# Two loads move behind two transposes, and 14 short idle products become 6 long ones

## The chip, the cores and the metric

The kernel runs on one core of a Trainium2 chip. The metric is the device time of one execution in microseconds. All times below are microseconds unless ns is written. The core has TensorE (PE, with its weight loads as PEld), VectorE (DVE), ScalarE (ACT), GpSimd (POOL) and SyncE (SP), each with an instruction stream of its own that it takes in order, and 16 DMA engines. A DMA is issued from one of the streams; here nearly all come from SyncE's.

## What is computed

Eight batches of retention (attention with a decaying causal mask, no softmax) with 8 heads, 576 positions and 64 values a head, and behind it a two-layer network over the 4608 tokens, in which the activation is a "snake":

```python
scores = scale * np.matmul(q, k.transpose(0, 1, 3, 2))
Dmat = np.where(rel >= 0, gamma[:, None, None] ** rel[None, :, :], 0.0)
attn = np.matmul(scores * Dmat, v)                 # (8, 8, 576, 64)
x = attn.transpose(0, 2, 1, 3).reshape(4608, 512)
h = x @ w_in                                       # (4608, 2048)
s = np.sin(alpha * h)
out = (h + s * s / (alpha + 1e-09)) @ w_out        # (4608, 512)
```

Inputs and output are float32; the kernel computes in float16 with float32 sums.

## The kernel before

**Tiles.** The first 512 positions of each batch form one block of 512 tokens; the last 64 positions of all batches form a ninth block. A batch's q, k and v come in two parts of 256 positions (`p` = 0, 1), each a float32 tile "raw" of 128 x 1024, in 512 KB. `load(b, nm, p)` issues one such load from SyncE (L148). `cast(b, nm, p, eng)` multiplies it by the decay factors into a float16 tile, on VectorE or GpSimd (L194; v is only copied, L121 or L119).

**Retention of a batch.** `crossed(b, p, nms)` issues a DMA transpose of the cast k or q from SyncE (L217), which gives the tiles kT and qT. `scores` multiplies kT and qT on TensorE (L372, 16 narrow products a call), and `masked` applies the decay mask on VectorE (L384). `outer` makes the sums of k times v for the four chunks of 128 positions (L308, narrow products), `evict` copies them to the tile kvs on ScalarE (L119), `more(c)` adds up the state from chunk to chunk on GpSimd (two instructions, L353 and L354), and `to_state(c)` writes the float16 state: on GpSimd (L346; for chunk 3 into the tile sS, which the ninth block uses) or on ScalarE (L344). There is one buffer kvs for all batches. `values` (L414) and `add_states` (L436) make the output of the batch, and `keep` copies it to xT.

**The network.** `project(n, fc, tag)` multiplies xT of block n with 128 columns of w_in in four wide products (L549) into the PSUM bank that the tag names. `sine` (L557, ScalarE), `square` (L568 on VectorE or GpSimd, L566 on ScalarE: the sine's output times itself) and `product` (L573, VectorE) make the activation gT; the product is the last reader of the bank, so the next project with the same tag waits for it. `gemm2` multiplies gT with w_out, four wide products a call (L592), and `finish(n, c, eng)` copies 128 tokens of output to osb (L119 or L121) and stores them in two DMAs from SyncE (L585).

**Order.** Up to the end of block 2's projections the order is written out by hand, call by call, in the program's text (L653 to L1131); after that a loop places the work of the later batches between the 16 units of each block (L1135 on). Each engine, and SyncE with its DMAs, works through its own instructions in the order of the text. Two places matter here.

At the start, `keep_busy(n, tag, m)` gives TensorE n products of m columns of zeros (L605), whose result nobody reads. One such call stands between the cast of the first q and its transposes on TensorE (`turn`, L227), which write to the same bank "h2".

In the middle (L994 to L1044), batch 3's retention starts while block 1's output and block 2's projections are under way. SyncE's stream there holds, in this order: the transposes of batch 3's second half, the loads of batch 4's k (second half) and q (first half), the transposes of batch 3's first half, the stores of block 1's output parts 1 and 0, and the loads of batch 4's k (first half), q (second half) and v. GpSimd's stream holds: the casts of batch 3's k (first half, in two parts), `more(3)` of batch 2, the casts of the two loads named, `to_state(3)` of batch 2, then `more(1)` to `more(3)` of batch 3 with their states. VectorE's holds: the two masks of batch 3's second half, the copy for `finish(1, 1)`, square and product of (2, 3) and of (2, 1), the mask of part (0, 1), square and product of (2, 7), the products of (2, 2) and (2, 11), and the cast of batch 4's q (second half). ScalarE's holds: the sines of (2, 3) and (2, 1), `evict` of batch 3 into kvs, the copy for `finish(1, 0)`, and the next sines.

Of the kernel before, what the change touches and what calls it, by code (L numbers as in the profile page):

```python
# [35 lines left out]
def kernel(  # L36
# [68 lines left out]
    V, A_, G_ = nc.vector, nc.scalar, nc.gpsimd  # L105
# [8 lines left out]
    def halves(n):  # L114
        return slice(64 * n, 64 * n + 64)
# [10 lines left out]
    def place(tag, shape, dtype):  # L126

        name = tag + next(slot_of[tag])
        if name not in places:
            places[name] = work.tile(shape, dtype, tag=name, bufs=1, name=name)  # L130
        return places[name]
# [5 lines left out]
    def load(b, nm, p):  # L137
        if p < 2 and b >= HALVED and nm != "q":
            t_ = place("raw", [P, H, 2 * D], F32)
            for g in range(2):  # L140
                for r in range(2):
                    s0 = 256 * p + 128 * g + 64 * r
                    nc.sync.dma_start(
                        t_[halves(g), :, r * D : r * D + D], src[nm][b, :, s0 : s0 + 64, :].rearrange("h i d -> i h d")
                    )
        elif p < 2:
            t_ = place("raw", [P, H, 2 * D], F32)
            nc.sync.dma_start(  # L148
                t_, src[nm][b, :, 256 * p : 256 * p + 256, :].rearrange("h (i r) d -> i h (r d)", r=2)
            )  # L150
        else:
            if b % 2 == 0:
                raw[b, nm, 2] = work.tile([P, H, D], F32, tag="raws", bufs=3, name=nm + "s32")
            t_ = raw[b - b % 2, nm, 2]
            nc.sync.dma_start(t_[halves(b % 2)], src[nm][b, :, 512:576, :].rearrange("h i d -> i h d"))
        raw[b, nm, p] = t_
# [47 lines left out]
    def new_T(b, nm, p):  # L204
        if (b, nm, p) not in T:
            T[b, nm, p] = (
                place(nm + "T", [P, 8, P], F16)
                if p < 2
                else work.tile([P, 4, P], F16, tag=nm + "Ts", bufs=B // 2, name=nm + "Ts")
            )  # L210
        return T[b, nm, p]

    def crossed(b, p, nms="kq"):
        for nm in nms:
            x = half[b, nm, p]
            x = x.rearrange("p a r t d -> p (a r t d)") if p < 2 else x.rearrange("p a t d -> p (a t d)")
            nc.sync.dma_start_transpose(new_T(b, nm, p), x)  # L217
# [363 lines left out]
    def finish(n, c, eng=None, cols=slice(0, 512), issue=(nc.sync, nc.sync)):  # L581
        osb = work.tile([P, 512], F32, tag="osb", bufs=4, name="osb")
        copy(eng or nc.scalar, osb[:, cols], ops[n, c, cols.start][:, cols])
        for r in range(2):
            issue[r].dma_start(rows_of(n, c)[r, :, cols], osb[halves(r), cols])  # L585

    def gemm2(n, u, tag, cols=slice(0, 512)):
        c, part = divmod(u, 4)
        if (n, c, cols.start) not in ops:
            ops[n, c, cols.start] = psum.tile([P, 512], F32, tag=tag, bufs=1, name="ops")  # L590
        for fk in range(4 * part, 4 * part + 4):
            matmul(  # L592
                ops[n, c, cols.start][:, cols], gT[n][:, fk, c * P : (c + 1) * P], w_out16[:, fk, cols],
                start=(fk == 0), stop=(fk == FC - 1), skip_group_check=True,
            )
# [6 lines left out]
    def keep_busy(n, tag, m=512):  # L602
        idle = psum.tile([P, 512], F32, tag=tag, bufs=1, name="idle")
        for _ in range(n):
            matmul(idle[:, 0:m], zero[:, 0:P], zero[:, 0:m], start=True, stop=True)  # L605
# [46 lines left out]
    with tc.manual_schedule():  # L652
# [20 lines left out]
        at[0].take_sum(0, A_)  # L673
        at[0].to_state(0, A_)
        cast(0, "q", 0, V)
        keep_busy(14, "h2", 200)
        at[0].next_sum(1)
        at[0].to_state(1, A_)
        load(0, "k", 1)
# [314 lines left out]
        at[2].more(3)  # L994
        crossed(3, 1, "k")
        crossed(3, 1, "q")
        load(4, "k", 1)
        cast(4, "k", 1, G_)
        load(4, "q", 0)
        cast(4, "q", 0, G_)  # L1000
        at[3].scores(1, 1, "m1")
        at[3].masked(1, 1)
        at[3].scores(1, 0, "m0")
# [3 lines left out]
        at[3].masked(1, 0)  # L1007
        crossed(3, 0, "k")
        crossed(3, 0, "q")
        gemm2(1, 7, "h1")  # L1010
        finish(1, 1, V)
        project(2, 1, "h0")
# [243 lines left out]
```

## Time and profile before

| | us |
|---|---|
| median of 3 runs | 306.36 |
| lowest, highest | 305.94, 307.76 |
| the profiled execution, its own time | 307.47 |
| its span, first to last instruction | 305.8 |
| TensorE busy in the span | 291.5 |
| VectorE, ScalarE, GpSimd busy | 199.9, 193.2, 128.7 |

The mean granted clock of TensorE is 0.998. In the lines of the trace, a row of a timeline gives the start, the time it took, the engine, the line of the kernel, the operation, the tiles written and read, the shape and the count of instructions merged; in brackets stand the idle time of the engine before it and what ended that. "SPq" is SyncE's stream, whose rows are DMA issues: their time is that of issuing, not of the transfer. "issue" means a wait without a cause in the profile. The end of a product in a row is modelled and includes its way through the array, so a next product can start before it.

### The profile page before, as it was taken

Reading aid. Unit: us, or ns where it says so; the run is one execution under the profiler, and the core shown is the slowest. Engines: PE = TensorE matmul, PEld = TensorE weight load, DVE = VectorE, ACT = ScalarE, POOL = GpSimd, SP = SyncE. Lnnn points to the kernel's source line nnn. Section 1 sums busy time; section 2 is a strip of 40 time slices with the busy share of each in tenths; the row PEclk is TensorE's granted clock in tenths of the full one; section 3 lists DMA queues with packets and bytes.
Section 4 is the critical chain, followed back from the end, with each engine's and each line's share of the span. In section 5 each row is a group of like instructions: output and inputs, shape, how many; then the busy total and the mean of one; then the engine's idle time right before and its main releaser. Section 6 shows DMA issues by size and latency. Waiting matters only on the chain.

```text
span 305.8 us, 7881 instructions
## 1 busy us (share of the span) xinstructions
PE 291.5 (95%) x3217; PEld 155.8 (51%) x3217; DVE 199.9 (65%) x281; ACT 193.2 (63%) x323; POOL 128.7 (42%) x149
## 2 busy tenths in 40 slices
PE   3879999999899999999999999999999999999995
PEld 1658555545444644554456444545455454444443
DVE  2877786978776876767667766566656746555600
ACT  3749886995378668664776577746774556555411
POOL 2767672468574555786159626743030000000000
PEclk9999999999999999999999999999999999999999
DMA  8999999998957379989799969966351121111232
GB/s 220 347 226 213 261 270 304 292 272 166 221 150 212 82 168 193 255 182 145 170 259 161 204 147 274 172 138 156 87 121 39 39 45 35 36 34 34 48 88 73
DMA packets 115620, 49.98 MB, mean 163 GB/s; under 512 B 71424, under 2 KB 110592, under 8 KB 115584
## 3 DMA queue, kind: packets, MB, share of 16 engines
q1 hardware_dynamic: 112064, 45.10, 62.5%
q0 software_dynamic: 2688, 4.19, 7.6%
q8 instruction: 25, 0.41, 0.6%
q10 hardware_dynamic: 832, 0.18, 0.4%
q14 instruction: 11, 0.09, 0.1%
HBM read 36.75 MB, written 9.44 MB: 151 GB/s over the span
## 4 chain that ended last, share of the span: by engine, by line
PE 83%; DMA 9%; DVE 3%; issue 2%; SPq 1%; ACT 1%; POOL 1%; DVEq 0%; POOLq 0%; ACTq 0%
PE ops L592 38%; PE hps L549 37%; DMA w_in<-in_moe_w_in_dram 3%; PE o L414 2%; PE sc L372 2%; DMA raw<-in_k_dram 2%; DMA raw<-in_q_dram 2%; DMA raw<-in_v_dram 2%; PE kv L308 1%; SPq L148 1%; PE o L436 1%; DVE ss L568 1%; DVE gT L573 1%; POOL k L194 1%; DVE ret L384 0%
## 5 line engine op out<-in xcount | busy, mean ns | idle before, releaser
L592 PE MATMUL ops<-w_out,gT 128*128 128x512 f16 (+2 forms) x592 | 142.8, 374 | 0.9 <-issue 0.7
L557 ACT ACTIVATE s<-hps,alpha_t 128x512 f16<-128x512 f32 x144 | 97.6, 684 | 67.3 <-PE hps L549 66.2
L573 DVE SCALAR_TENSOR_TENSOR gT<-ss,inva,hps 128x512 f16<-128x512 f16 x144 | 105.5, 745 | 52.5 <-ACT ss L566 48.1
L549 PE MATMUL hps<-xT,w_in 128*128 128x512 f16 (+1 forms) x544 | 126.8, 367 | 0.3 <-DMA w_in<-in_moe_w_in_dram 0.2
L549 PEld LDWEIGHTS <-w_in 128*128 128x128 f16 x608 | 67.9, 114 | 56.7 <-issue 1.0
L592 PEld LDWEIGHTS <-gT 128*128 128x128 f16 x592 | 56.3, 98 | 63.9 <-issue 1.7
L568 DVE TENSOR_TENSOR ss<-s 128x512 f16<-128x512 f16 x62 | 37.1, 598 | 18.0 <-ACT s L557 17.4
L566 ACT ACTIVATE ss<-s 128x512 f16<-128x512 f16 x73 | 46.0, 631 | 1.4
L194 POOL TENSOR_TENSOR k<-raw,cn 128x1024 f16<-128x1024 f32 (+1 forms) x17 | 26.6, 1574 | 38.0 <-DMA raw<-in_k_dram 30.5
L119 ACT COPY osb<-ops 128x512 f32<-128x512 f32 (+1 forms) x33 | 19.2, 580 | 15.3 <-PE ops L592 14.0
L384 DVE TENSOR_TENSOR ret<-sc,mask 128x1024 f16<-128x1024 f32 x20 | 23.8, 1218 | 4.2 <-PE sc L372 4.1
L194 POOL TENSOR_TENSOR q<-raw,cn 128x1024 f16<-128x1024 f32 (+1 forms) x10 | 18.2, 1837 | 3.4 <-DMA raw<-in_q_dram 3.4
L354 POOL TENSOR_TENSOR kvs<-s,kvs 128x256 f32<-128x256 f32 x21 | 16.6, 790 | 3.6 <-ACT kvs L119 2.3
L353 POOL TENSOR_TENSOR s<-kvs,cn 128x256 f32<-128x256 f32 x21 | 12.8, 612 | 8.6 <-ACT kvs L119 8.4
L121 POOL CAST v<-raw 128x1024 f16<-128x1024 f32 (+1 forms) x11 | 11.0, 997 | 13.0 <-DMA raw<-in_v_dram 13.0
L549 PE MATMUL hps<-xS,w_in 128*128 128x512 f16 x64 | 16.4, 379 | 0.0
L119 ACT CAST xT<-o 128x1024 f16<-128x1024 f32 (+1 forms) x13 | 12.7, 986 | 5.4 <-PE o L436 5.3
L568 POOL TENSOR_TENSOR ss<-s 128x512 f16<-128x512 f16 x9 | 9.3, 1037 | 8.6 <-ACT s L557 8.6
L119 ACT COPY kvs<-kv 128x512 f32<-128x512 f32 (+2 forms) x14 | 8.0, 573 | 7.4 <-PE kv L308 5.1
L178 POOL TENSOR_TENSOR ks<-ks,cn 128x512 f16<-128x512 f32 x4 | 4.2, 1042 | 19.8 <-DMA vs<-in_v_dram 12.3
L372 PE MATMUL sc<-qT,kT 64*64 64x128 f16 (+1 forms) x512 | 10.6, 215 | 1.8 <-DVE ret L384 1.0
L414 PE MATMUL o<-ret,v 64*64 64x128 f16 (+1 forms) x512 | 11.4, 215 | 0.8 <-issue 0.3
(57 smaller groups left out, 153.2 us busy)
## 6 DMA issues: line engine op xcount, KB each, us to landing
out_dram<-osb SPq DMA_DIRECT2D x70, 128.0 KB, 2.5
raw<-in_q_dram SPq DMA_DIRECT2D x16, 512.0 KB, 5.9
raw<-in_k_dram SPq DMA_DIRECT2D x10, 512.0 KB, 6.1
raw<-in_v_dram SPq DMA_DIRECT2D x10, 512.0 KB, 5.9
raw<-in_v_dram SPq DMA_DIRECT2D x24, 128.0 KB, 3.4
raw<-in_k_dram SPq DMA_DIRECT2D x24, 128.0 KB, 3.3
w_in<-in_moe_w_in_dram POOLq DMA_DIRECT2D x4, 512.0 KB, 11.5
w_out<-in_moe_w_out_dram POOLq DMA_DIRECT2D x4, 512.0 KB, 11.7
```

Of the source, the lines that this page charges most:

```text
L119: eng.copy(d_, s_)
L194: eng.tensor_tensor(dst[:, a0:a1].rearrange("p a r t d -> p t (a r) d"), t_.rearrange("p (t a) x -> p t a x", t=2)[:, :, a0:a1].rearrange( ...
L354: nc.gpsimd.tensor_tensor(self.kvs[:, c], s32, self.kvs[:, c], ADD)
L372: matmul(sc[halves(g), t, c : c + n], kT[halves(t), 2 * a + r, halves(g)], qT[halves(t), 2 * a : 2 * a + 2, 64 * g + i0 : 64 * g + 64], st ...
L384: nc.vector.tensor_tensor(ret.rearrange("p t (z x) -> p (t z) x", z=2)[:, :, 0:n], sc.rearrange("p t (z x) -> p (t z) x", z=2)[:, :, 0:n], ...
L414: made.append(matmul(o[t][halves(e), c : c + 128].rearrange("p (r i) -> p r i", r=2)[:, :, i0:64], v16[halves(g), 4 * t + 2 * x + e, r, :] ...
L549: matmul(hps_of[n, fc][0][:, cols], w_in16[fc // 4][:, a, fc % 4 :: 4], xs[n][:, a, cols], start=(a == 0 and part != 1), stop=(a == KT - 1 ...
L557: nc.scalar.activation(s_t, hps, mybir.ActivationFunctionType.Sin, bias=0.0, scale=alpha_t[:, fc : fc + 1],)
L566: nc.scalar.activation(ss_t, s_t, mybir.ActivationFunctionType.Square)
L568: eng.tensor_tensor(ss_t, s_t, s_t, MULT)
L573: nc.vector.scalar_tensor_tensor(gT[n][:, fc, :], ss_t, inva[:, fc : fc + 1], hps, MULT, ADD)
L592: matmul(ops[n, c, cols.start][:, cols], gT[n][:, fk, c * P : (c + 1) * P], w_out16[:, fk, cols], start=(fk == 0), stop=(fk == FC - 1), sk ...
```

## The change

Two edits. The first swaps, in the text of the order, two loads of batch 4 with their casts on GpSimd against what stood between them and `gemm2(1, 7)`: they now come behind the two DMA transposes of batch 3's first half, and on GpSimd behind `to_state(3)` of batch 2. The buffers that they use stay the same. The second replaces 14 idle products of 200 columns by 6 of 467.

```diff
         at[0].to_state(0, A_)
         cast(0, "q", 0, V)
-        keep_busy(14, "h2", 200)
+        keep_busy(6, "h2", 467)
         at[0].next_sum(1)
...
         at[2].more(3)
         crossed(3, 1, "k")
         crossed(3, 1, "q")
-        load(4, "k", 1)
-        cast(4, "k", 1, G_)
-        load(4, "q", 0)
-        cast(4, "q", 0, G_)
         at[3].scores(1, 1, "m1")
         at[3].masked(1, 1)
         at[3].scores(1, 0, "m0")
         at[2].to_state(3, G_)
         project(2, 3, "op")
         sine(2, 3)
         at[3].masked(1, 0)
         crossed(3, 0, "k")
         crossed(3, 0, "q")
+        load(4, "k", 1)
+        cast(4, "k", 1, G_)
+        load(4, "q", 0)
+        cast(4, "q", 0, G_)
         gemm2(1, 7, "h1")
         finish(1, 1, V)
         project(2, 1, "h0")
```

## The prediction

> **What bounds the kernel now.** I read the page first: the engines' shares and the DMA queues.
>
> ```profile
> span 305.8 us, 7881 instructions
> ...
> PE 291.5 (95%) x3217; PEld 155.8 (51%) x3217; DVE 199.9 (65%) x281; ACT 193.2 (63%) x323; POOL 128.7 (42%) x149
> ...
> q8 instruction: 25, 0.41, 0.6%
> ```
>
> TensorE is busy for 95% of the span. So an edit pays only if it removes a place where TensorE stands still, or makes one. The moved loads lie between 72 and 97 us, so next I read the chain of work that ended last for that stretch, and then each engine's timeline in it.
>
> ```profile
> 82.22 1.79 DVE ss L568
> ...
> 88.04 5.56 DMA raw<-in_q_dram
> ...
> 93.79 1.22 DVE q L194
> ...
> 101.03 0.54 PE kv L308 x64
> ```
>
> The chain leaves TensorE here. It runs through a VectorE square that took 1.79 us and, later, through the load of batch 4's q (second half), which VectorE must cast before it can make its next product. What TensorE lost by it is seen in its own timeline.
>
> ```profile
> 82.09 0.71 PE L308 MATMUL kv<-v,k 64*64 64x64 f16 x64
> 83.65 0.42 PE L372 MATMUL sc<-qT,kT 64*64 64x128 f16 x16 [0.85 <-DMA qT<-q]
> 84.00 2.98 PE L549 MATMUL hps<-xT,w_in 128*128 128x512 f16 x12
> 86.81 3.62 PE L592 MATMUL ops<-w_out,gT 128*128 128x512 f16 x16
> 90.27 3.62 PE L549 MATMUL hps<-xT,w_in 128*128 128x512 f16 x16
> 93.72 1.89 PE L592 MATMUL ops<-w_out,gT 128*128 128x512 f16 x8
> 95.72 1.02 PE L549 MATMUL hps<-xT,w_in 128*128 128x512 f16 x4
> 96.68 0.42 PE L414 MATMUL o<-ret,v 64*64 64x128 f16 x16
> ```
>
> Sixteen wide products go from 90.27 to the next start at 93.72: 0.216 each, with nothing lost. With that step the standstills are: 83.65 - (82.09 + 0.54 for 64 narrow products, the chain's row of 101.03) = 1.02; 86.81 - (84.00 + 12 x 0.216) = 0.22; 95.72 - (93.72 + 8 x 0.216) = 0.27; 96.68 - (95.72 + 4 x 0.216) = 0.10. Their sum, 1.6 us, is the most that moving the loads can give here.
>
> **The change, part one: two loads move behind two transposes.** First SyncE's queue, which the four transfers share.
>
> ```profile
> 68.52 1.25 SPq L217 DMA_TRANSPOSE qT<-q  x1
> ...
> 74.82 0.58 SPq L148 DMA_DIRECT2D raw<-in_k_dram  x1
> ...
> 76.12 2.93 SPq L217 DMA_TRANSPOSE kT<-k  x1
> 79.14 2.39 SPq L217 DMA_TRANSPOSE qT<-q  x1
> ```
>
> Then GpSimd, whose stream also holds the two casts that move.
>
> ```profile
> 72.34 2.04 POOL L194 TENSOR_TENSOR k<-raw,cn 128x512 f16<-128x512 f32 x2
> ...
> 75.03 0.72 POOL L354 TENSOR_TENSOR kvs<-s,kvs 128x256 f32<-128x256 f32 x1
> 79.27 1.90 POOL L194 TENSOR_TENSOR k<-raw,cn 128x1024 f16<-128x1024 f32 x1 [3.51 <-PE sc L372]
> 81.82 1.90 POOL L194 TENSOR_TENSOR q<-raw,cn 128x1024 f16<-128x1024 f32 x1 [0.65 <-DMA raw<-in_q_dram]
> 83.68 0.80 POOL L346 TENSOR_TENSOR sS<-kvs,cn 128x256 f16<-128x256 f32 x1
> 85.60 0.61 POOL L353 TENSOR_TENSOR s<-kvs,cn 128x256 f32<-128x256 f32 x1 [1.13 <-ACT kvs L119]
> ```
>
> *Transposes.* Their source, batch 3's first half of k, is cast by 74.38 (72.34 + 2.04), so the first can issue at 74.82, where the load now does. A transpose right behind another took 1.25 (68.52) to 2.39 (79.14) of the queue. Two of them are issued by 77.3 to 79.6, instead of 81.53 (79.14 + 2.39). TensorE could use them at 82.63. The old issue, done at 81.53, let the scores start at 83.65, 2.1 later; with the upper row this is 81.7. So the wait of 1.02 goes with either.
>
> *Loads.* They issue from 77.3 to 79.6 on, instead of 74.82. The k load reached its cast 4.45 after its issue (74.82 to 79.27), the q load 2.55 behind it (81.82). So k comes at 81.8 to 84.1 and q at 84.3 to 86.6. I take 82.3 and 84.9: nearer the lower end, since 68.52 is a transpose with no load ahead of it, as these will be, but not at it, since a longer issue is as common.
>
> *GpSimd's order.* The state of batch 2 (sS) now comes ahead of the casts and runs at 75.8 (75.03 + 0.72) instead of 83.68. ScalarE waited for it:
>
> ```profile
> 84.51 1.02 ACT L119 COPY kvs<-kv 128x1024 f32<-128x1024 f32 x1 [1.63 <-POOL sS L346]
> 85.42 0.59 ACT L119 COPY osb<-ops 128x512 f32<-128x512 f32 x1
> ...
> 88.98 1.05 ACT L344 ACTIVATE s<-kvs,cn 128x64 f16<-128x64 f32 x4
> 91.33 0.69 ACT L557 ACTIVATE s<-hps,alpha_t 128x512 f16<-128x512 f32 x1 [1.30 <-PE hps L549]
> ```
>
> That copy of kvs can now start at about 82.9, when the 64 products are done. What follows in ScalarE's order comes 1.6 earlier: the copy of the output block (85.42 to 83.8), SyncE's stores of it, and behind these the load of 88.04, now at 86.4. VectorE's cast of that q moves from 93.79 to 92.2, and the standstills of 0.27 and 0.10 are covered. What is late next: the state sums, queued on GpSimd behind the two casts, start at 84.9 + 1.9 = 86.8 instead of 85.60, at the upper end at 88.5. A sum is two instructions (0.61, and 0.72 as at 75.03), done by 89.9 at the latest. ScalarE needs it for the work of 88.98, which would shift by 0.9, and 1.30 of idle time follow: no cost.
>
> *VectorE.* Here lies the price.
>
> ```profile
> 82.14 1.86 DVE L568 TENSOR_TENSOR ss<-s 128x512 f16<-128x512 f16 x1
> 84.04 0.75 DVE L573 SCALAR_TENSOR_TENSOR gT<-ss,inva,hps 128x512 f16<-128x512 f16 x1
> 84.70 0.42 DVE L568 TENSOR_TENSOR ss<-s 128x512 f16<-128x512 f16 x1
> 85.16 0.75 DVE L573 SCALAR_TENSOR_TENSOR gT<-ss,inva,hps 128x512 f16<-128x512 f16 x1
> ```
>
> The same square takes 0.42 at 84.70 and 1.86 at 82.14. The long one lies under GpSimd's cast of 81.82 to 83.72 and ends 0.28 after it: it waited for the cast. The product behind it, done at 84.79, frees the bank for the 5th of the wide products of 84.00, and the next one, done at 85.91, that for the 9th. So with the DMA wait gone TensorE still meets these two. The Trainium skill ("SBUF — State Buffer", section "Who interferes with whom") has this as a rule: a VectorE instruction with two SBUF inputs and a GpSimd instruction that reads SBUF exclude each other for the whole instruction, and the first to start wins. The trace agrees at 82.14.
>
> So the sum turns on who starts first. With k's cast at 82.3 the square passes ahead of it (82.14 to 82.56) and its product ends at 83.4. The second square meets that cast (82.3 to 84.2), ends at 84.5, and its product at 85.2. TensorE makes the scores at 82.63, four products from 83.0 and four from 83.87, is ready for the 9th at 84.73 and waits 0.5 until 85.25. Of 1.6 remain 0.5: gain **1.1**. Bounds: 1.6 gained, if k lands after 83.4 and both squares pass first; 1.2 lost, as the first rival works out.
>
> **Part two: 14 idle products of 200 columns become 6 of 467.**
>
> ```profile
> 8.27 2.52 PE L605 MATMUL idle<-zero 128*128 128x200 f16 x14
> 10.84 0.61 PE L227 MATMUL tr<-ident,q 128*128 128x128 f16 x8
> ```
>
> 2800 columns become 2802; at 2.52 us for 2800 the six take the same time, and the transposes behind them still start at 10.84. These eight take 0.61 together, the clock is up by then, and with the same busy time ahead it should be so again. Cost 0. What remains is that TensorE's stream has 8 products and 8 weight loads fewer, and the trace shows where this may count.
>
> ```profile
> 19.27:196.09 176.82, 174.17 (x2168) 94.55 (x2168) 130.96 (x175) 127.19 (x214) 105.95 (x114) 1.00 0.91 208
> ```
>
> ```profile
> 19.28 0.36 PE L414 MATMUL o<-ret,v 64*64 64x128 f16 x11 [0.30 <-issue]
> ```
>
> ```profile
> 194.13 1.24 PE L592 MATMUL ops<-w_out,gT 128*128 128x512 f16 x5
> 196.10 0.81 PE L592 MATMUL ops<-w_out,gT 128*128 128x512 f16 x3 [0.72 <-issue]
> ```
>
> Two waits of TensorE have no releaser ("issue"). The one at 196.10 costs 196.10 - (194.13 + 5 x 0.216) = 0.89. The instruction queue moved 25 packets, 0.41 MB / 25 = 16.4 KB each, and 6434 products and loads / 25 make 257 to a packet. Between the two waits lie 2 x 2168 = 4336 of them: 17 packets of 255. So both waits stand at a seam between two blocks of instructions. With 16 instructions fewer ahead, the second seam falls 16 later in the code, behind 8 more wide products: it is reached at 195.21 + 8 x 0.216 = 196.94. The block was there at 196.10 and is asked for a few tenths later at most, so the wait goes: gain **0.89**. Bounds: 0, if the block comes later too, and a loss of the same 0.89, if another seam lands badly. The seam of 19.28 moves by 8 short products, a tenth or two: 0.
>
> **Sum.** 1.1 + 0.89 = 2.0 off the profiled execution's 307.47 (span 305.8 and 1.7 around it) gives 305.5. That execution is 1.1 above the median of 306.36, so against the median: **304.4**.
>
> **Rivals.**
> *The cast comes first, twice.* If k lands by 82.0, its cast takes 82.0 to 83.9 and holds the first square until 84.2; that product ends at 84.95. If q then lands by 84.6, its cast (to 86.5) holds the second square until 86.8 and the product until 87.5. TensorE, ready at 83.87, waits 1.1, then, ready at 85.85, 1.7: 2.8 against 1.6, a loss of 1.2. With the seam's gain: 306.36 + 1.2 - 0.89 = 306.7, slower than before. It decides where k lands: before or after 82.14, and my 82.3 is barely past it. For it: the lower row gives 81.8. Against: 2.39 is seen for a transpose behind another too (79.14).
> *The seam stays.* The wait at 196.10 has another cause, or turns up elsewhere: 306.36 - 1.1 = 305.3. The Trainium skill ("Runtime: NRT & Kernel Launch", section "Instruction fetch mechanics") has blocks of 256 instructions and calls the cost of crossing from one to the next mostly hidden. By that rule the shorter stream is worth nothing; the 0.89 speaks against it.
> *The loads come late.* With 2.93 (76.12) for each transpose, q lands near 87.7, the sums end past 91, and ScalarE's next sine starts 0.8 late: taken as the whole gain of part one, 305.5.
>
> **How the numbers follow.** Likeliest (square first, seam gone) 0.45: 304.4, own range 303.8 to 304.9. Cast first 0.22: 306.7. Seam stays 0.11: 305.3. Loads late 0.07: 305.5. Beyond these, waits that I did not see, 0.15. The range 303.5 to 307.1 holds the likeliest, the two milder rivals and nearly all of the first: 8 in 10. Over 1% (about what a measurement of this kernel can tell from no change) is below 303.3 or above 309.4. The four priced cases stay inside that, and even their upper bounds together (1.6 + 0.89 = 2.5) do. So the tails are the 0.15 and a little of the cases' own: 0.12 faster, 0.07 slower, 0.81 within.
>
> **What would show it.** In the changed profile: the transposes of batch 3's first half issue at 74.8 and about 76.2; the scores at 82.6 without a wait for qT; sS on GpSimd at 75.8; ScalarE's copy of kvs at 82.9; a square of 0.42 at 82.1, or of 1.9 if the cast was first; no "issue" wait at 196. A 9th wide product later than 86, or an "issue" wait in another burst, would make the prediction wrong.

## The result and the profile after

| | before | after |
|---|---|---|
| median of 20 executions of each, us | 306.39 | 307.72 |
| ratio | | 1.0055, interval 1.0033 to 1.0076 |
| profiled execution, its own time | 307.47 | 310.0 |
| its span | 305.8 | 308.3 |

The changed kernel is slower by about 0.55% (1.3 us between the medians). The forecast was 304.4 with a range of 303.5 to 307.1: wrong in sign and outside its range. Ratios here and below are formed from undisturbed executions alone, so they can differ a little from the ratio of the medians shown.

The page of the changed kernel, the lines that answer to those of before:

```profile
span 308.3 us, 7863 instructions
...
PE 293.0 (95%) x3209; PEld 155.2 (50%) x3209; DVE 200.9 (65%) x281; ACT 193.5 (63%) x323; POOL 129.3 (42%) x149
```

TensorE has its 8 products fewer and yet more busy time and a longer span. Next its own timeline around the moved loads:

```profile
83.31 0.71 PE L308 MATMUL kv<-v,k 64*64 64x64 f16 x64
83.90 0.42 PE L372 MATMUL sc<-qT,kT 64*64 64x128 f16 x16
84.25 1.05 PE L549 MATMUL hps<-xT,w_in 128*128 128x512 f16 x4
86.28 1.02 PE L549 MATMUL hps<-xT,w_in 128*128 128x512 f16 x4 [0.98 <-DVE gT L573]
88.32 1.86 PE L549 MATMUL hps<-xT,w_in 128*128 128x512 f16 x4 [1.02 <-DVE gT L573]
89.98 4.43 PE L592 MATMUL ops<-w_out,gT 128*128 128x512 f16 x16
94.25 3.62 PE L549 MATMUL hps<-xT,w_in 128*128 128x512 f16 x16
97.70 1.89 PE L592 MATMUL ops<-w_out,gT 128*128 128x512 f16 x8
99.43 1.03 PE L549 MATMUL hps<-xT,w_in 128*128 128x512 f16 x4
100.38 0.42 PE L414 MATMUL o<-ret,v 64*64 64x128 f16 x16
```

The wait of the scores for the transpose is gone. Of the two small standstills at the end that of 0.27 is gone too: from 94.25 to 97.70 sixteen products took 3.45, and from 97.70 to 99.43 eight took 1.73, each 0.216. That of 0.10 is still there, as 100.38 - (99.43 + 4 x 0.216) = 0.09; the same stands in before between the wide products of 81.13 and the narrow ones of 82.09, where nothing is waited for, so it was no gain to be had. In place of what went stand two waits for VectorE's products: with the step of 0.216 they are 86.28 - (84.25 + 4 x 0.216) = 1.17 and 88.32 - (86.28 + 4 x 0.216) = 1.18. That is 2.3 us here, against 1.5 before (the 1.6 without the 0.10). GpSimd and VectorE show why:

```profile
77.07 0.61 POOL L346 TENSOR_TENSOR sS<-kvs,cn 128x256 f16<-128x256 f32 x1
83.26 1.90 POOL L194 TENSOR_TENSOR k<-raw,cn 128x1024 f16<-128x1024 f32 x1 [5.58 <-DMA raw<-in_k_dram]
85.12 2.08 POOL L194 TENSOR_TENSOR q<-raw,cn 128x1024 f16<-128x1024 f32 x1
```

```profile
83.36 2.08 DVE L568 TENSOR_TENSOR ss<-s 128x512 f16<-128x512 f16 x1
85.48 0.75 DVE L573 SCALAR_TENSOR_TENSOR gT<-ss,inva,hps 128x512 f16<-128x512 f16 x1
86.14 1.34 DVE L568 TENSOR_TENSOR ss<-s 128x512 f16<-128x512 f16 x1
87.52 0.75 DVE L573 SCALAR_TENSOR_TENSOR gT<-ss,inva,hps 128x512 f16<-128x512 f16 x1
```

The cast of k started at 83.26, 0.10 ahead of the first square, and the square lasted until 85.44, 0.28 after the cast's end at 85.16. The cast of q followed without a gap, and the second square ended at 87.48, again 0.28 after it (87.20). Without a cast beside it such a square takes 0.42. Each product that follows a square frees a bank, so each delay reaches TensorE.

Now the second edit. The places without a releaser ("issue") in TensorE's timeline are these:

```profile
20.02 0.25 PE L414 MATMUL o<-ret,v 64*64 64x128 f16 x3 [0.74 <-issue]
...
47.79 0.36 PE L436 MATMUL o<-qT,s 64*64 64x128 f16 x12 [1.22 <-issue]
```

The wait of 0.72 that stood at 196.10 is not there, as forecast. But the wait of 0.30 at 19.28 has become one of 0.74, and at 47.79 there is one of 1.22 in a burst of narrow products where before had none. That is 1.22 + 0.44 against 0.72: by these rows alone the second edit loses 0.9 in this execution. Some of the delay is taken up behind them, at places where TensorE had waited for others in before and which it now reaches later: 0.6 at 38 to 40, of which this row of before has the most, and 0.2 at 60.

```profile
38.23 0.45 PE L308 MATMUL kv<-v,k 64*64 64x64 f16 x32 [0.28 <-POOL v L121]
```

Last, the clock. Three stretches of the changed kernel, with the busy time of the engines, the granted clock (PEclk), the DMA share and rate:

```profile
84.00:88.30 4.30, 2.32 (x26) 1.10 (x24) 4.23 (x5) 2.83 (x5) 4.22 (x4) 0.99 0.54 127
88.30:91.70 3.40, 3.38 (x9) 1.22 (x9) 1.86 (x2) 1.45 (x3) 3.16 (x6) 0.51 0.96 271
91.70:95.00 3.30, 3.30 (x17) 1.59 (x16) 3.20 (x5) 1.41 (x5) 1.76 (x3) 1.00 1.12 333
```

For 3.4 us right behind the two waits the granted clock was 0.51. The four products from 88.32 to 89.98 took 0.80 more than 4 x 0.216, the sixteen from 89.98 to 94.25 took 0.81 more than 16 x 0.216: 1.6 us. The mean granted clock is 0.994 or less in this and in five more of the 20 executions, and the other 14 have a median of 307.62. So the clock explains 1.6 of the 2.3 us by which 310.0 lies above the median of 307.72, and next to nothing of the difference between the medians. With that, the profiled execution's 2.5 more of span (308.3 - 305.8) has these terms: +0.8 (2.3 against 1.5 around the moved loads), +1.6 (the clock), +0.9 (the waits without a cause), and -0.8 at the places just named.

### The profile page after: what moved, and what is told of

It is laid out like the page before. It is cut to its first block, busy times and chain, and to the rows that moved or that the text cites. A ratio compares the mean times of both kernels' runs of the same rounds, so it can differ in the third digit from the quotient of the medians.

```text
span 308.3 us, 7863 instructions
## 1 busy us (share of the span) xinstructions
PE 293.0 (95%) x3209; PEld 155.2 (50%) x3209; DVE 200.9 (65%) x281; ACT 193.5 (63%) x323; POOL 129.3 (42%) x149
## 4 chain that ended last, share of the span: by engine, by line
PE 89%; POOL 2%; DVE 2%; DMA 2%; issue 2%; SPq 1%; ACT 1%; DVEq 0%; POOLq 0%; ACTq 0%
PE ops L592 41%; PE hps L549 40%; PE o L414 3%; PE sc L372 2%; DMA raw<-in_k_dram 2%; PE kv L308 1%; POOL w_in L109 1%; DVE ss L568 1%; PE o L436 1%; SPq L148 1%; PE tr L227 1%; POOL k L194 1%; POOL q L194 1%; DVE gT L573 0%; DVE ret L384 0%
## 5 line engine op out<-in xcount | busy, mean ns | idle before, releaser
L568 DVE TENSOR_TENSOR ss<-s 128x512 f16<-128x512 f16 x62 | 38.2, 616 | 18.4 <-ACT s L557 17.8
L119 ACT COPY osb<-ops 128x512 f32<-128x512 f32 (+1 forms) x33 | 19.2, 582 | 15.2 <-PE ops L592 14.0
L353 POOL TENSOR_TENSOR s<-kvs,cn 128x256 f32<-128x256 f32 x21 | 14.0, 665 | 12.2 <-ACT kvs L119 12.0
L354 POOL TENSOR_TENSOR kvs<-s,kvs 128x256 f32<-128x256 f32 x21 | 15.8, 753 | 3.8 <-ACT kvs L119 2.5
L549 PE MATMUL hps<-xS,w_in 128*128 128x512 f16 x64 | 16.4, 379 | 0.0
L178 POOL TENSOR_TENSOR ks<-ks,cn 128x512 f16<-128x512 f32 x4 | 4.2, 1044 | 22.8 <-DMA vs<-in_v_dram 11.5
L414 PE MATMUL o<-ret,v 64*64 64x128 f16 (+1 forms) x512 | 11.5, 215 | 1.2 <-issue 0.7
L346 POOL TENSOR_TENSOR s<-kvs,cn 128x256 f16<-128x256 f32 x17 | 10.8, 639 | 1.8 <-PE o L436 0.7
## 6 DMA issues: line engine op xcount, KB each, us to landing
w_in<-in_moe_w_in_dram POOLq DMA_DIRECT2D x4, 512.0 KB, 11.5
```

The costliest lines, as they stand in the source:

```text
L119: eng.copy(d_, s_)
L353: nc.gpsimd.tensor_tensor(s32, self.kvs[:, c - 1], g1.unsqueeze(2).to_broadcast([P, 4, D]), MULT)
L354: nc.gpsimd.tensor_tensor(self.kvs[:, c], s32, self.kvs[:, c], ADD)
L414: made.append(matmul(o[t][halves(e), c : c + 128].rearrange("p (r i) -> p r i", r=2)[:, :, i0:64], v16[halves(g), 4 * t + 2 * x + e, r, :] ...
L549: matmul(hps_of[n, fc][0][:, cols], w_in16[fc // 4][:, a, fc % 4 :: 4], xs[n][:, a, cols], start=(a == 0 and part != 1), stop=(a == KT - 1 ...
L568: eng.tensor_tensor(ss_t, s_t, s_t, MULT)
```

## The experiments

The theory to test had two parts. First: the move is good for about 1 us, but only if the squares pass ahead of the casts; with a cast first it costs. Second: which waits without a cause appear is set by where the blocks of TensorE's instructions end, so by how many instructions stand ahead, not by the length of the idle products. The rivals: the move costs by itself (its loads later, its queue longer); the 467 columns cost by themselves; or all of it is the place of the seams.

The kernels were measured in three groups of four, each beside its own executions of the kernel before, whose medians were 307.05, 307.21 and 306.92. "Standstills" sums what TensorE stood still from 17 to 206 us in the profiled execution (behind that it is 1.3 to 1.6 in all of them): the difference between each product's start and the next, less 0.216 for 512 columns, half of it for 256 and 0.03 for a narrow one, counted where it is over 0.03. The span less this sum is 293.1 to 293.8 in all 14 profiles, so the spans differ by TensorE's standstills and by nothing else over some tenths (time lost to a lower clock is counted in them). "80 to 93" is the part of the sum from that stretch, where the squares and casts lie. Of e8_late_idle10 there are nine executions, of the others of a group twelve.

| kernel | loads moved | casts or squares | idle products | median | ratio to before, interval | span | standstills | 80 to 93 |
|---|---|---|---|---|---|---|---|---|
| before | no | | 14 x 200 | | | 305.8 | 12.2 | 1.4 |
| after | yes | | 6 x 467 | 307.72 | 1.0055 (1.0033 to 1.0076) | 308.3 | 14.7 | 4.4 (1.6 clock) |
| e1_move_only | yes | | 14 x 200 | 308.77 | 1.0040 (1.0007 to 1.0072) | 307.5 | 14.0 | 2.2 |
| e2_idle_only | no | | 6 x 467 | 306.49 | 0.9976 (0.9944 to 1.0008) | 304.3 | 11.0 | 1.1 |
| e3_after_pad8 | yes | | 6 x 467 and 8 x 64 | 307.74 | 1.0005 (0.9974 to 1.0036) | 305.9 | 12.5 | 2.0 |
| e4_idle10 | no | | 10 x 280 | 306.25 | 0.9964 (0.9939 to 0.9989) | 305.2 | 11.9 | 1.3 |
| e5_after_sqA | yes | squares on ScalarE | 6 x 467 | 306.16 | 0.9981 (0.9960 to 1.0002) | 304.0 | 10.9 | 0.4 |
| e6_before_sqA | no | squares on ScalarE | 14 x 200 | 306.80 | 1.0000 (0.9977 to 1.0022) | 304.3 | 11.1 | 1.1 |
| e7_cast_late | yes | casts later | 6 x 467 | 306.36 | 0.9979 (0.9962 to 0.9997) | 304.7 | 11.5 | 0.5 |
| e8_late_idle10 | yes | casts later | 10 x 280 | 304.88 | 0.9949 (0.9931 to 0.9968) | 305.0 | 11.2 | 0.5 |
| e9_after_idle10 | yes | | 10 x 280 | 307.50 | 0.9993 (0.9962 to 1.0025) | 306.2 | 13.0 | 2.4 |
| e10_late_idle14 | yes | casts later | 14 x 200 | 305.76 | 0.9961 (0.9940 to 0.9982) | 303.7 | 10.2 | 0.3 |
| e11_after_again | yes | | 6 x 467 | 308.33 | 1.0045 (1.0020 to 1.0069) | 307.0 | 13.6 | 2.4 |
| e12_move_again | yes | | 14 x 200 | 307.54 | 1.0018 (0.9996 to 1.0040) | 305.6 | 12.2 | 2.0 |

Four profiles have a standstill that the others do not have, at places far from both edits: TensorE waits for GpSimd's stream at 162 in e3_after_pad8 (0.6) and e9_after_idle10 (1.1), and for a gT at 131 in e1_move_only and e11_after_again (0.5 to 0.6). They are part of the standstills of these four.

### The two edits apart: e1_move_only and e2_idle_only

The first keeps the move and the 14 old idle products, the second makes only the edit of the idle products.

```diff
 e1_move_only, against after
-        keep_busy(6, "h2", 467)
+        keep_busy(14, "h2", 200)
 e2_idle_only, against before
-        keep_busy(14, "h2", 200)
+        keep_busy(6, "h2", 467)
```

> Only the two loads move; the 14 idle products of 200 stay. Theory 1 (the move costs by the port lock, the idle edit by seams between blocks of instructions): the two squares on VectorE wait for GpSimd's casts as in the changed kernel, TensorE stands 1.1 and 1.2 before its 5th and 9th wide product behind 84, against 1.6 in all before: 0.7 slower than before, about 307.1, ratio 1.002. The waits without a cause are those of the kernel before: 0.3 at 19.3 and 0.7 to 0.9 at 196, none at 47. Theory 2 (the move is the whole of the loss): 307.7, ratio 1.0055 or more, since the shorter stream would be worth something between 0 and 0.9. Theory 3 (the idle edit is the whole of the loss): 306.4, ratio 1.000.

> Only the idle products change (6 of 467), the loads stay. Theory 1: the wait at 196 goes (0.89 gained), a wait of 1.2 without a cause stands at 47.8 among the short products with the state, and the one at 19 to 20 grows by some 0.4 to 0.6 and is met by the first projection: 0.7 to 1.1 slower, about 307.3, ratio 1.003; TensorE's wait of 1.0 for qT at 83 to 85 stays, and the squares' long time of 1.86 stays with it. Theory 2 (the move is the whole of the loss): 305.5 to 306.4, ratio 0.997 to 1.000. Theory 3: 307.7, ratio 1.0055.

Measured: the move alone 1.0040 (1.0007 to 1.0072), slower; the idle products alone 0.9976 (0.9944 to 1.0008), not slower, where theory 1 had 1.003. VectorE in e1_move_only:

```profile
83.33 1.53 DVE L568 TENSOR_TENSOR ss<-s 128x512 f16<-128x512 f16 x1
...
85.55 1.35 DVE L568 TENSOR_TENSOR ss<-s 128x512 f16<-128x512 f16 x1
```

Both squares are long again, with the old idle products: the loss belongs to the move. In e2_idle_only the wait near 196 is gone, and both new waits are there:

```profile
19.81 0.25 PE L414 MATMUL o<-ret,v 64*64 64x128 f16 x3 [0.80 <-issue]
```

```profile
46.74 0.36 PE L436 MATMUL o<-qT,s 64*64 64x128 f16 x12 [0.35 <-issue]
```

So these can come with the idle products alone. Here the one at 46.74 was 0.35 and not 1.22: the same place, another size. And e1_move_only, with the old idle products, shows that the place is not new:

```profile
45.24 1.10 PE L414 MATMUL o<-ret,v 64*64 64x128 f16 x44
47.11 0.25 PE L414 MATMUL o<-ret,v 64*64 64x128 f16 x4 [0.78 <-issue]
```

It waits with 4 products of the burst L414 left, where after has 4 products of the next burst done (12 left): 8 products apart, as many as the idle products are fewer. So a seam seems to lie here in each of these kernels, and the edit changes where in the burst it falls and how often it costs. Of the profiles with 14 idle products or their count of instructions (before and five of the experiments) one shows a wait here, of the three with 10 two, of the five with 6 all.

### Length or number of the idle products: e3_after_pad8 and e4_idle10

The first adds eight narrow idle products at the very start of the changed kernel, so that as many instructions stand ahead of the later code as before, with the products of 467 columns kept. The second changes their number to 10 in the kernel before.

```diff
 e3_after_pad8, against after
         keep_busy(3, "op")
+        keep_busy(8, "op", 64)
 e4_idle10, against before
-        keep_busy(14, "h2", 200)
+        keep_busy(10, "h2", 280)
```

> The changed kernel, with 8 more idle products of 64 columns right behind the first three, where TensorE waits for the first load anyway (from 2.7 to 6.7). The count of TensorE's instructions is that of the kernel before again, while the 6 products of 467 stay. If the place of the seams is the cause, the waits without a cause are back where they were before (0.3 at 19.3, 0.7 to 0.9 at 196) and the one at 47.8 is gone, and the time is that of the kernel in which only the loads move, about 307.1 (ratio 1.002). If the length of the idle products is the cause, the waits stay at 20.0 and 47.8 and the time at 307.7 (1.0055).

> The kernel before with 10 idle products of 280 columns in place of 14 of 200: the same 2800 columns, 8 instructions fewer instead of 16. By the seams: at 196 the block is asked for 4 wide products later, 0.86 of the 0.89, so that wait goes to 0 to 0.1; at 47 the seam moves by half of the way, and the wait there is 0 if the block comes as early as in the kernel before, up to 1.2 if it comes as late as in the changed one; the wait at 19.3 grows by 0.0 to 0.3. So 305.5 to 306.6, ratio 0.997 to 1.001. If the length of the products counts, half of the changed kernel's loss: 307.0.

TensorE's waits without a cause in e3_after_pad8:

```profile
19.21 0.36 PE L414 MATMUL o<-ret,v 64*64 64x128 f16 x11 [0.30 <-issue]
```

```profile
196.29 0.81 PE L592 MATMUL ops<-w_out,gT 128*128 128x512 f16 x3 [0.38 <-issue]
```

With the old number of instructions the waits at 19.2 and 196 are back, at the same instruction of the same burst as before (11 narrow products left of the one, 3 wide products of the other), and none stands near 47, although the products of 467 columns are kept. The number of instructions ahead sets where TensorE waits, not the length of the idle products. In e4_idle10, where 4 products and 4 weight loads fewer stand ahead, the same seam has 7 products of its burst left in place of 11, 4 fewer, and the one near 47 stands right between two bursts, 4 behind that of e1_move_only:

```profile
19.30 0.30 PE L414 MATMUL o<-ret,v 64*64 64x128 f16 x7 [0.31 <-issue]
```

```profile
47.38 0.42 PE L436 MATMUL o<-qT,s 64*64 64x128 f16 x16 [1.00 <-issue]
```

So the number counts one for one. Counted over all 14 profiles, TensorE has exactly 445, 1211 or 4781 of its own products and loads behind it at each of these waits (near 19, 47 and 196).

The traces also show what ends them. The DMA queue "instruction" moves its 25 packets one by one, and each of the 27 waits at these three places ends 1.25 to 1.47 us after the end of one of these packets: in before at 19.28 and 196.10, with packets that ended at 17.87 and 194.72; in after at 20.02 and 47.79, with packets that ended at 18.68 and 46.35. Where no wait stands at one of the three places, TensorE came to it 1.66 us or more after the packet. At the place near 47 in before the packet had ended at 44.63 and TensorE came at 46.29. So these are waits for a block of instructions, and their size goes by when the block's packet comes and when TensorE gets to its first instruction.

Even with this wait of 1.00 e4_idle10 took 0.9964 of before (0.9939 to 0.9989); the one at 196 is gone in it. What e3_after_pad8 gained over after is not settled, since the two come from different groups.

### Take away the contention: e5_after_sqA with its control e6_before_sqA

In both, the squares of (2, 3) and (2, 1) go from VectorE to ScalarE, right behind their sines; e6_before_sqA does the same to the kernel before, since the change of engine may have an effect of its own.

```diff
         sine(2, 3)
+        square(2, 3, A_)
...
         sine(2, 1)
+        square(2, 1, A_)
...
-        square(2, 3, V)
         product(2, 3)
...
-        square(2, 1, V)
         product(2, 1)
```

> The changed kernel, with the two squares of (2, 3) and (2, 1) on ScalarE, each right behind its sine, instead of VectorE. If the cost of the move is the exclusion between VectorE's squares and GpSimd's casts, both products come in time for the 5th and the 9th wide product behind the scores of batch 3, TensorE's waits of 1.1 and 1.2 there go, and 1.8 to 2.3 of the changed kernel's time with them: 305.4 to 306.0, ratio to the kernel before 0.994 to 0.999. If the move costs by something else (later loads, the order of the DMAs), the time stays near 307.7, ratio 1.004 or more.

> The kernel before with the same two squares on ScalarE: the control. Its wait of 1.0 for qT is not touched by that; the waits of 0.2, 0.27 and 0.1 behind it may go. By the exclusion the time falls by 0.2 to 0.6 only, ratio 0.998 to 0.999, and the changed kernel with its squares on ScalarE is then faster than this one by 0.5 to 1.5, where with the squares on VectorE it is slower. By the other theory this falls as much or as little as the changed kernel does.

e5_after_sqA took 0.9981 (0.9960 to 1.0002), the control 1.0000 (0.9977 to 1.0022). TensorE in e5_after_sqA, and then in the control:

```profile
83.82 2.78 PE L549 MATMUL hps<-xT,w_in 128*128 128x512 f16 x12
86.44 3.62 PE L592 MATMUL ops<-w_out,gT 128*128 128x512 f16 x16
```

```profile
83.35 0.42 PE L372 MATMUL sc<-qT,kT 64*64 64x128 f16 x16 [0.69 <-DMA qT<-q]
```

With the squares out of the way the twelve wide products run through (86.44 - 83.82 = 2.62 = 12 x 0.218), although the casts are where the change put them. The control still has the wait for qT, which the move takes away. So neither the later loads nor the longer queue costs anything here: the squares beside the casts do. The move of the squares alone shows no gain.

### Let the squares go first: e7_cast_late and e8_late_idle10

The two casts on GpSimd go behind the first state sum of batch 3, which waits for ScalarE's copy of kvs; the loads stay where the change put them. The second has 10 idle products of 280 columns besides.

```diff
 both, against after
         load(4, "k", 1)
-        cast(4, "k", 1, G_)
         load(4, "q", 0)
-        cast(4, "q", 0, G_)
...
         at[3].more(1)
+        cast(4, "k", 1, G_)
+        cast(4, "q", 0, G_)
         finish(1, 0)
 e8_late_idle10 besides
-        keep_busy(6, "h2", 467)
+        keep_busy(10, "h2", 280)
```

> The changed kernel, with the two casts of batch 4's k and q behind the first state sum of batch 3 on GpSimd, so that they start some 3 later, at about 86.5; the loads stay where the change put them. By the exclusion the square at 83.4 takes 0.42 and the one behind it some 0.4 to 0.6; TensorE's two waits go to 0 to 0.4: 305.5 to 306.1, ratio 0.995 to 0.999. If the loads' later landing is what costs, the same time as the changed kernel or more, 307.7.

> The same, with 10 idle products of 280 columns, which alone gave 0.9964. If the waits at the seams and the exclusion are all there is, TensorE keeps only the wait without a cause at 47 (0 to 1.2): 304.8 to 305.8, ratio 0.993 to 0.998, the fastest so far. If the casts so late make VectorE or ScalarE wait for the states of batch 3, TensorE waits between 90 and 104 instead, and the gain is gone: 306.4.

Measured: 0.9979 (0.9962 to 0.9997) and 0.9949 (0.9931 to 0.9968). VectorE and GpSimd in e7_cast_late:

```profile
83.39 0.41 DVE L568 TENSOR_TENSOR ss<-s 128x512 f16<-128x512 f16 x1
...
84.51 0.42 DVE L568 TENSOR_TENSOR ss<-s 128x512 f16<-128x512 f16 x1
...
87.81 1.01 DVE L568 TENSOR_TENSOR ss<-s 128x512 f16<-128x512 f16 x1 [0.97 <-ACT s L557]
```

```profile
85.26 0.61 POOL L353 TENSOR_TENSOR s<-kvs,cn 128x256 f32<-128x256 f32 x1 [7.54 <-ACT kvs L119]
...
86.63 1.91 POOL L194 TENSOR_TENSOR k<-raw,cn 128x1024 f16<-128x1024 f32 x1
88.50 2.09 POOL L194 TENSOR_TENSOR q<-raw,cn 128x1024 f16<-128x1024 f32 x1
```

The squares take 0.41 and 0.42, and TensorE has no standstill over 0.35 between 21 us and the end but the one at 47.8. The casts are 3.4 later (86.63 against 83.26) and TensorE waits nowhere for them. The state sums come earlier by it (85.26 against 87.17), but they are not what the gain needs: e5_after_sqA has no long wait either, with its casts ahead of the sums. The cast now meets a later square, at 87.81: it takes 1.01 and ends at 88.82, 0.28 after the cast (88.54), and this one TensorE does not feel. GpSimd's idle time of 7.54 ahead of the sum shows that it had the time. e8_late_idle10 has the like squares (0.42 and 0.42); its profiled execution is the slowest of its nine, with a granted clock of 0.50 from 18.4 to 21.8.

### Both places of the casts on one chip: e9 to e12

The first two groups and the first measurement had left the effects on different chips. The last group puts the two places of the casts and the kinds of idle products side by side: the changed kernel and the move alone once more (e11_after_again, e12_move_again), and two new ones, of which one has after's casts with 10 idle products, and the other the later casts with the old idle products.

```diff
 e9_after_idle10, against after
-        keep_busy(6, "h2", 467)
+        keep_busy(10, "h2", 280)
 e10_late_idle14, against e7_cast_late
-        keep_busy(6, "h2", 467)
+        keep_busy(14, "h2", 200)
```

> The changed kernel with 10 idle products of 280 columns in place of 6 of 467; the casts keep their place in the change, ahead of the square. Theory (the cost is the order of cast and square): the square is held by the cast as in the changed kernel, 1.9 to 2.1 us at 83, the two waits of TensorE for gT between 84 and 89 stay, 2 us together, and the time is about 2 us (ratio 0.006) above the kernel with the casts moved later and the same 10 products (304.9 beside 307.2 of before): ratio to before about 1.001. Rival (the cost of the change is the place of the seams alone): with 10 products it is as good as that kernel, ratio 0.995.

> The loads moved as in the change, the casts behind the first state sum of batch 3, and the 14 idle products of 200 columns kept. Theory: the gT waits between 84 and 89 are gone, the wait near 196 to 198 without a cause is back (0.8). So it is about 2 us (0.006) below the move with the casts in their place (1.004 in its run), ratio about 0.997 to 0.999. Rival (the move gains nothing wherever the casts stand): 1.002 or more.

> The changed kernel again, unaltered, beside the three others on one chip. Theory: both gT waits, a wait near 48 and none at 196; ratio 1.003 to 1.007 as measured first. In those of its runs in which the granted clock falls behind the waits (0.51 for 3.4 us in the profile), the time is 1.6 us or more above its others; without such runs about 1.001 to 1.004.

> The move of the loads alone again, 14 idle products of 200 columns. Theory: both gT waits, the wait near 197 of 0.8; ratio 1.002 to 1.006 as in its first run (1.004, interval 1.0007 to 1.0072). If the idle products are worth nothing at all, it equals the changed kernel run beside it within 0.002; if the wait at 196 is a gain that other seams do not take back, it is 0.003 above.

The steps between the medians are: before 306.92; the move with the casts ahead of the squares 307.54 (+0.6, in an interval that includes no change); with the casts later 305.76 (-1.2). So the order of casts and squares is worth 1.8 us, and the intervals of the two do not meet. The profiles give 2.0 against 0.3 for the stretch from 80 to 93, a difference of 1.7. VectorE in e12_move_again and in e9_after_idle10, and the cast in each:

```profile
81.97 1.45 DVE L568 TENSOR_TENSOR ss<-s 128x512 f16<-128x512 f16 x1
...
84.12 1.34 DVE L568 TENSOR_TENSOR ss<-s 128x512 f16<-128x512 f16 x1
```

```profile
81.23 1.91 POOL L194 TENSOR_TENSOR k<-raw,cn 128x1024 f16<-128x1024 f32 x1 [4.95 <-PE ops L592]
```

```profile
81.89 1.93 DVE L568 TENSOR_TENSOR ss<-s 128x512 f16<-128x512 f16 x1
...
84.52 1.34 DVE L568 TENSOR_TENSOR ss<-s 128x512 f16<-128x512 f16 x1
```

```profile
81.64 1.90 POOL L194 TENSOR_TENSOR k<-raw,cn 128x1024 f16<-128x1024 f32 x1 [5.43 <-DMA raw<-in_k_dram]
```

In both, TensorE waits as in after; in e9_after_idle10:

```profile
84.65 1.02 PE L549 MATMUL hps<-xT,w_in 128*128 128x512 f16 x4 [0.83 <-DVE gT L573]
86.70 1.03 PE L549 MATMUL hps<-xT,w_in 128*128 128x512 f16 x4 [1.02 <-DVE gT L573]
```

The cast leads the square by 0.74 in the one, by 0.25 in the other, by 0.10 in after. The square lasts 1.91 + 0.28 less the lead: 1.45, 1.93 (1.90 + 0.28 - 0.25) and 2.08. The second square is 1.34 or 1.35 in all of them, since the cast of q runs right behind. So the length of the square follows from the lead to a hundredth.

The idle products: 467 columns against 200, with the casts in their place, 308.33 against 307.54, +0.8, though the intervals of the two (1.0020 to 1.0069, 0.9996 to 1.0040) overlap. In the profile of e11_after_again the wait near 48 is there again:

```profile
48.08 0.36 PE L436 MATMUL o<-qT,s 64*64 64x128 f16 x12 [1.46 <-issue]
```

With the casts later the same two kinds gave 0.9979 and 0.9961 (in two groups), and alone 467 columns gave 0.9976. So by these ratios the edit of the idle products lies somewhere between a gain of 0.7 and a loss of 0.8 us, the intervals are wider still, and none of the runs settles its sign. Ten products of 280 columns were below the 14 of 200 in all three settings (0.9964 against 1; 0.9949 against 0.9961; 0.9993 against 1.0018), by 0.4 to 1.1 us; only the first of these is clear by its interval.

For e9_after_idle10 some 2 us above the kernel with later casts were expected, and by the ratios (0.9993 against 0.9949) it is 1.4, with both waits for gT in its profile and no wait at all at 47; so the seams alone are not the cost (the wait of 1.1 at 162 is in its profile too). Its twelve executions spread from 305.3 to 308.9, wider than those of the three others beside it; whether the square came first in the shorter ones no trace shows. That e11_after_again came with a granted clock of 0.998 in its profile, with the same two waits, shows that these alone don't bring the clock down. Three of its twelve executions have a clock of 0.992 to 0.994; they took 308.7 to 309.8, the others 306.9 to 308.9, so the gap of 1.6 or more that was expected of them is not there throughout.

The traces show what differs. The granted clock changes only at steps of 3.41 us: in after it is at 1 for 22 of them (75.1 us), then at 0.5 for one. The step ahead of that drop, from 84.79 to 88.20, holds nearly all of both waits for gT, and TensorE is busy for 1.53 of it. In e1_move_only and e12_move_again one step holds both waits too, but the first wait is half as long and TensorE is busy for 1.96 and 2.04; in the three others a step ends before the waits are over, and the poorest has 2.46. The only other drop between 10 and 300 us is that of e8_late_idle10, without such waits: the step ahead of it, from 14.98 to 18.39, has 1.63. Every other step between 10 and 300 us, in all 14 profiles, has 1.95 or more and was followed by the full clock. That this share decides is argued from two drops; where between 1.63 and 1.95 the line would lie no run shows.

The best measured are e8_late_idle10 at 0.9949 (0.9931 to 0.9968) and e10_late_idle14 at 0.9961 (0.9940 to 0.9982), both faster than both kernels of this case; between the two the intervals don't decide.

## Why the prediction was wrong

**What was right.** The changed kernel is 1.22 late at this place, for the waits at 20 and 48 (its 64 narrow products start at 83.31, before's at 82.09). With that taken off the transposes issued at 74.4 and 75.8 (forecast 74.8 and 76.2), sS ran at 75.85 (75.8), ScalarE copied kvs at 82.92 (82.9) and the scores started at 82.68 (82.6) without a wait:

```profile
75.65 1.23 SPq L217 DMA_TRANSPOSE kT<-k  x1
76.98 1.26 SPq L217 DMA_TRANSPOSE qT<-q  x1
78.30 0.58 SPq L148 DMA_DIRECT2D raw<-in_k_dram  x1
```

```profile
84.14 1.02 ACT L119 COPY kvs<-kv 128x1024 f32<-128x1024 f32 x1
```

The standstill of 0.27 was covered (that of 0.10 was none, so the forecast's 1.6 was 1.5), the wait at 196 went, and the square came out as one of the two kinds that the forecast had for it.

**The step that failed in part one: "I take 82.3 and 84.9" for the landing of k and q.** The two transposes took 1.23 and 1.26 of the queue, both as the row of 1.25, so the load issued at 78.30 - 1.22 = 77.1, even ahead of the 77.3 of the lower bound. It took 4.96 to its cast in place of 4.45, and the cast started at 83.26 - 1.22 = 82.04, not at 82.3; the square was ready at 82.14. The forecast had put the load by the side of the bounds (81.8 to 84.1) on which the square wins, by 0.16, on the ground that the longer issue of 2.39 was as common; but the rows of 2.39 and 2.93 were issued just behind the two loads, and in the moved order none stand there. The row of 68.52 was the like case, and the forecast said so and did not follow it. That likeness was not proof (at 72.58 a transpose of before took 2.19 with no load right ahead of it), but the runs bear it out: in the ten profiles with the loads moved the two transposes took 1.23 to 1.46 and 1.25 to 1.26, in the four with the loads in their old place 2.62 to 2.93 and 1.47 to 2.39. In all six profiles with the casts in their changed place the cast came first, by 0.10 to 0.74, so it is no toss. The first rival, "the cast comes first, twice", is what happened. It had 1.1 and 1.7 for the two waits; measured were 1.17 and 1.18, since q's cast could follow at once (q had landed) and so ended at 87.20 - 1.22 = 85.98, 0.5 earlier than the rival had it (86.5). The Trainium skill ("SBUF — State Buffer", section "Who interferes with whom") has the exclusion as a rule: whoever starts first keeps the other out to the end of its instruction. The traces agree for a cast that starts first: in each pair shown here the square ends 0.28 after the cast.

**What part one would have been.** 1.1 was forecast for a first square that passes and a second that meets the cast; no run here has that. For both squares ahead of the casts the forecast had its bound of 1.6. e10_late_idle14 is that case and gains 1.2 (306.92 to 305.76; by its interval 0.6 to 1.8). So the move can gain about what the forecast had for it, under a condition that the change did not meet.

**The step that failed in part two: "so the wait goes: gain 0.89", with the other seams at nothing.** The wait at 196 went, in every kernel with fewer instructions ahead. But moving one seam moves all 25, and the forecast priced the others only by "the seam of 19.28 moves by 8 short products, a tenth or two: 0" and as a bound. TensorE did come to that seam only some tenths later, but its block came 0.8 later as well (its packet ended at 18.68, in before at 17.87), and that was the term put at nothing. The wait at 19.28 went from 0.30 to 0.74, and the seam near 47, which costs nothing in the profile of before and 0.78 in one of five others with its count of instructions, took 0.35 to 1.46 in all five with 6 products. The bound "a loss of the same 0.89, if another seam lands badly" named the mechanism. The second rival had the wait turn up elsewhere, but priced that at no gain and not at a loss. The "issue" wait in another burst, which the forecast gave as a sign of being wrong, came. That the waits are tied to the place in the stream is shown by e1_move_only, e3_after_pad8 and e4_idle10, and that they end on the coming of a block by the times of the packets. What the two new waits cost in the median is less sure: the interval of e2_idle_only (0.9944 to 1.0008) does not exclude the forecast's gain. The Trainium skill ("Runtime: NRT & Kernel Launch", section "Instruction fetch mechanics") calls the cost of crossing a block mostly hidden. That holds for most of the 25 here; at the two or three where TensorE has just had a run of narrow products it waited 0.3 to 1.5.

**The sum.** By the last group: part one +0.6 in place of -1.1, part two about +0.8 (not settled) in place of -0.89; together +1.4 in place of -2.0. The first measurement has +1.3. The upper end of the range, 307.1, held the first rival only with the seam's gain in it; both steps failed at once.

**"Cost 0" for the clock at the start** came out, but not for the reason given. The six products took the same 2.52, yet the eight transposes behind them took 1.01 in place of 0.61, so the clock rose later:

```profile
11.01 1.01 PE L227 MATMUL tr<-ident,q 128*128 128x128 f16 x8
...
13.09 0.62 PE L227 MATMUL tr<-ident,q 128*128 128x128 f16 x8 [0.21 <-DVE q L194]
```

```profile
12.90 0.62 PE L227 MATMUL tr<-ident,q 128*128 128x128 f16 x8 [0.68 <-DVE q L194]
```

The wait for VectorE's cast in front of the next transposes covered it: 0.68 in before (the second fence), 0.21 in after. It is no mark of the wide products: with 14 of 200 columns e10_late_idle14 had the same 1.01. The drop to 0.51 behind the two waits for gT, in one of the six profiles that have such waits, was not foreseen.

**What stays open.** The wait near 47 is missing in e9_after_idle10 and there in e8_late_idle10, whose TensorE has the same instructions: the block's packet ended at 44.44 in the one and at 46.87 in the other. What makes the packet come sooner or later is not shown. And it is open whether part two is worth anything by itself.

## What to carry to other kernels

When a load is moved later, look at what its consumer on GpSimd will meet on VectorE at the new time: here 0.1 us decided between a square of 0.42 and one of 2.1, and the way out is not a faster load but the consumer's place in GpSimd's stream, since that engine had 7.5 us to spare. A landing time must be taken from the row whose queue looks like the new order, and where two candidates lie on both sides of a threshold the nearer likeness should carry the forecast, not the middle. A change in the number of instructions on TensorE shifts every seam behind it, so a wait that it removes at one must be set against those that it can make or lengthen at all the others, first of all in bursts of narrow products.

## What the runs showed of the hardware

The square's end is the cast's end plus 0.28 in each of the five pairs shown, with leads of the cast from 0.10 to 1.18 us. That is less than the 0.41 to 0.42 of a square by itself.

TensorE's waits without a releaser came at a fixed place in the instruction stream (e1_move_only, e3_after_pad8 and e4_idle10, to the instruction) with a size that varied from one execution to the next, from nothing to 1.46 us at the place near 47. At three places in 14 profiles each of the 27 waits ended 1.25 to 1.47 us after the end of a 16.4 KB packet of the queue "instruction".

The granted clock fell to 0.51 for 3.4 us behind two standstills of 1.17 and 1.18 us, in a stretch of 4.30 us with 2.32 of it busy. Five other profiles with two such standstills (0.5 to 1.0 and 1.2) kept a mean clock of 0.998 or more. Between 10 and 300 us of 14 traces the clock fell only behind the two steps of 3.41 us in which TensorE was busy least, 1.53 and 1.63 us; the next had 1.95 and kept it.
